# Clustered attention and a gated MLP: score and maxima matmuls over 128 partitions instead of 80 or 81, and a new list of operations

## The chip, the cores and the metric

The kernel runs on one core of a Trainium2 chip. The metric is the device time of one execution in microseconds (us). The core has TensorE (PE, with its weight loads shown apart as PEld), VectorE (DVE), ScalarE (ACT), GpSimd (POOL) and SyncE (SP), which issues nearly all transfers. Each engine works through its own queue in order.

## The reference

Four batches of eight heads with 768 positions of 64 dimensions. Each query and each key is put into one of 16 clusters (the nearest centroid by cosine). A query attends only to keys of its own cluster. The result goes through an MLP with a spatial gate.

```python
q_assign = np.argmax(np.einsum('bhsd,hcd->bhsc', q_n, c_n), axis=-1)
k_assign = np.argmax(np.einsum('bhsd,hcd->bhsc', k_n, c_n), axis=-1)
mask = q_assign[:, :, :, None] == k_assign[:, :, None, :]
scores = np.where(mask, scale * np.matmul(q, k.transpose(0, 1, 3, 2)), -1000000000.0)
attn = np.exp(scores - np.max(scores, axis=-1, keepdims=True))
attn = attn / (np.sum(attn, axis=-1, keepdims=True) + 1e-09)
x = np.matmul(attn, v)                 # heads side by side: (4, 768, 512)
h = np.maximum(x @ w_in, 0.0)
u, v = (h[..., :d_ff // 2], h[..., d_ff // 2:])
v_n = (v - mu) / np.sqrt(var + 1e-06)
v_s = np.einsum('ts,bsd->btd', w_spatial, v_n) + b_spatial[None, :, None]
out = (u * v_s) @ w_out
```

## The kernel before

The heads are taken in 16 pairs (four to a batch), and each head of a pair is a unit of attention. For a pair, `prep` (L604, for the first pair `prep0`, L546) loads keys and queries transposed (`raw`), splits them into a half-precision high part and a low part, and finds the clusters: small matmuls with the centroids (L570 to L572, L632 to L634, L644), then five VectorE steps (L664 to L669) and two that write a one-hot row for each cluster into `ohx` (L677, L678). SP transposes `ohx` into `oht` (L679) and copies its rows into the operand tile (L690).

That operand tile, `hq`, has 128 partitions and three slots of two heads by 768 positions. Slot 0 holds the keys' high part in partitions 0 to 63 and in 64 to 79 the keys' one-hot rows, partition 80 a constant row. Slot 1 holds the queries' high part, the queries' one-hot rows in 64 to 79, and from 80 on up to three shift rows, which are written later: they carry each query's maximum, so that the exponent needs no subtraction of its own. Slot 2 and the tile `lo` hold the operands with the low parts. Four tiles `hq` go round. The constants in the code are R_OH = 64, R_SH = 80, R_E = 81, R_END = 83.

For each unit, `shifts` (L739) forms the scores once to get the maxima: matmuls at L762 over partitions 0 to 79 (`0:R_SH`), each half (512 columns) or two quarters (2 x 256 columns) of a row block into one PSUM tile `acc`, of which there are four; VectorE reduces each to a maximum (L768). The maxima go as rows through `shx` and `sht` into `hq` (L795, L801; for the first pair through a matmul at L792). `attend` (L844) then forms the transposed scores: first the part with low parts over 128 partitions (L865), then the high part with one-hot and shift rows over 81 partitions (L867, `0:R_E`). ACT takes the exponent (L875) and the half-precision high part (L879), POOL the low part (L880), and TensorE sums with V (L885). Of the pairs 9, 11, 13 and 15 `attend_rows` (L806) does it by rows, without shifts: scores at L818 and L820 (the latter over 80 partitions), the maximum at L823.

When the four pairs of a batch are done, `mlp` (L942) follows: all its large matmuls are at L951, with 128 partitions and 512 columns, and fill TensorE beside the attention of the next batches.

The order is not made by a scheduler. The program first collects all operations with what they need, each with a number, and `Plan.run` issues them in the order of the list `ORDER` (L129, 3164 numbers). Each engine's queue, SP's included, is what that list leaves for it.

Of the kernel before, what the change touches and what calls it, by code (L numbers as in the profile page):

```python
# [8 lines left out]
F16 = mybir.dt.float16  # L9
# [6 lines left out]
P = 128  # L16
# [22 lines left out]
HQ_BUFS = 4  # L39
# [59 lines left out]
class Plan:  # L99
# [166 lines left out]
def kernel(  # L266
# [253 lines left out]
    def sp(fn, **k):  # L520
        return op("SP", fn, **k)
# [284 lines left out]
    def attend_rows(u):  # L806
# [5 lines left out]
        for t in range(NT):  # L812
# [3 lines left out]
            def scores(sc=sc, ts=ts):  # L816
                for cs in halves:
                    T.matmul(out=sc.t[:, cs], lhsT=hq.t[:, 2, h, ts], rhs=lo.t[:, h, cs], start=True, stop=False)  # L818
                for cs in halves:
                    T.matmul(out=sc.t[:, cs], lhsT=hq.t[0:R_SH, 1, h, ts], rhs=hq.t[0:R_SH, 0, h, cs], start=False, stop=True)  # L820
# [284 lines left out]
```

## Time and profile before

| | |
|---|---|
| median of 3 timed runs | 639.91 us (638.49 to 640.25) |
| the profiled execution, its own time | 643.21 us |
| span of its profile | 641.4 us |
| mean granted TensorE clock | 0.979 |
| DMA | 87.73 MB, mean 137 GB/s |
| costliest groups | POOL L880, 144 of 1706 ns; DVE L768, 216 of 681 ns; ACT L875, 144 of 900 ns; PE L951, 1296 of 379 ns |

A line of the profile names the engine, the line of the kernel, the operation, what it writes and reads, and its shape. Matmuls are pipelined: one of 512 columns lasts 379 ns by its record, but the next one starts earlier, so the distance from start to start tells its cost. "PEclk" is the share of its full clock that TensorE was granted. In a timeline the brackets at the end of a row give the idle time of the engine ahead of it and what ended it.

### The profile page before, as it was taken

How to read it: one execution, taken by the hardware profiler on the slowest of the kernel's cores; microseconds unless marked ns; L12 is line 12 of the kernel's file. 1: busy time of each engine (PE TensorE's matmuls, PEld its weight loads, DVE VectorE, ACT ScalarE, POOL GpSimd, SP SyncE). 2: the span in 40 equal slices, each digit the busy share in tenths (PEclk: the TensorE clock that was granted, in tenths of full speed). 3: DMA queues.
4: the chain of work that ended last, by engine and by line, in shares of the span. 5: the costliest groups of instructions: out<-in, count | busy, mean ns of one | idle time of the engine just before them, and what ended most of it. 6: DMA issues, size and time to landing. Idle time of an engine off the chain costs nothing.

```text
span 641.4 us, 16489 instructions
## 1 busy us (share of the span) xinstructions
PE 609.4 (95%) x6573; PEld 363.3 (57%) x6573; DVE 478.9 (75%) x994; ACT 446.6 (70%) x722; POOL 432.8 (67%) x309
## 2 busy tenths in 40 slices
PE   3889989889999999999999999999999999999997
PEld 2436666576666666546555575566556655544443
DVE  6997999999999997897779678669797665245220
ACT  6667989999987888747568587788769965022002
POOL 3453889998797889657657778588679887224210
PEclk9956999999999999999999999999999999999999
DMA  6556786677474656734989879888896189810145
GB/s 205 134 127 166 111 181 135 157 174 176 103 188 104 152 122 153 150 84 107 183 131 184 184 152 187 145 167 149 167 171 122 32 156 154 128 33 34 26 73 164
DMA packets 174812, 87.73 MB, mean 137 GB/s; under 512 B 158448, under 2 KB 161552, under 8 KB 174736
## 3 DMA queue, kind: packets, MB, share of 16 engines
q1 hardware_dynamic: 171136, 80.40, 62.0%
q10 hardware_dynamic: 3600, 6.30, 2.9%
q8 instruction: 51, 0.84, 0.6%
q14 instruction: 25, 0.20, 0.1%
HBM read 27.63 MB, written 6.29 MB: 53 GB/s over the span
## 4 chain that ended last, share of the span: by engine, by line
PE 72%; DVE 14%; ACT 4%; DMA 3%; issue 3%; POOL 1%; SPq 1%; ACTq 0%; DVEq 0%
PE acc L951 39%; PE acc L885 8%; PE acc L762 6%; DVE nm L768 5%; PE sc L865 5%; PE sc L867 5%; PE acc L834 4%; PE sc L818 2%; PE sc L820 2%; DMA xT<-wk 2%; DVE lo L544 1%; ACT wk L879 1%; DMA raw<-in_kqT_dram 1%; POOL wk L880 1%; ACT wk L875 1%
## 5 line engine op out<-in xcount | busy, mean ns | idle before, releaser
L880 POOL TENSOR_TENSOR wk<-wk,wk 128x768 f16<-128x768 f32 x144 | 242.4, 1706 | 42.7 <-ACT wk L879 30.7
L768 DVE TENSOR_REDUCE nm<-acc 128x1 f32<-128x512 f32 (+1 forms) x216 | 140.4, 681 | 25.3 <-PE acc L762 25.0
L875 ACT ACTIVATE wk<-sc,plog 128x768 f32<-128x768 f32 x144 | 127.7, 900 | 22.2 <-PE sc L867 16.5
L951 PE MATMUL acc<-win,xT 128*128 128x512 f16 x576 | 134.2, 379 | 0.1
L879 ACT CAST wk<-wk 128x768 f16<-128x768 f32 x144 | 116.7, 831 | 6.2 <-PE acc L885 3.4
L951 PE MATMUL acc<-vn,wsp 128*128 128x512 f16 x432 | 99.6, 379 | 1.0 <-DVE nm L768 0.9
L829 POOL TENSOR_TENSOR wk<-wk,wk 128x768 f16<-128x768 f32 x48 | 80.3, 1676 | 29.9 <-ACT wk L828 26.6
L885 PEld LDWEIGHTS <-wk 128*128 128x128 f16 x2592 | 90.1, 98 | 10.9 <-issue 1.1
L885 PE MATMUL acc<-vhl,wk 128*128 128x65 f16 (+1 forms) x2592 | 95.4, 194 | 0.2 <-POOL wk L880 0.2
L762 PE MATMUL acc<-hq 80*128 80x512 f16 (+1 forms) x288 | 82.4, 360 | 11.7 <-DVE nm L768 3.8
L951 PEld LDWEIGHTS <-xT 128*128 128x128 f16 x576 | 55.0, 97 | 62.1 <-issue 2.1
L865 PE MATMUL sc<-hq,lo 128*128 128x512 f16 (+1 forms) x288 | 72.5, 334 | 2.8 <-ACT wk L875 2.0
L867 PE MATMUL sc<-hq 81*128 81x512 f16 (+1 forms) x288 | 72.4, 333 | 0.0
L951 PEld LDWEIGHTS <-wsp 128*128 128x128 f16 x432 | 41.5, 98 | 47.9 <-issue 1.6
L823 DVE TENSOR_REDUCE nq<-sc 128x1 f32<-128x768 f32 x48 | 45.8, 954 | 28.8 <-PE sc L820 25.4
L951 PE MATMUL acc<-wou,wk 128*128 128x512 f16 x288 | 67.1, 379 | 0.0
L826 ACT ACTIVATE wk<-sc,nq 128x768 f32<-128x768 f32 x48 | 47.5, 990 | 24.6 <-DVE nq L825 5.8
L1014 POOL TENSOR_TENSOR wk<-u,wk 128x512 f16<-128x512 f32 x24 | 28.3, 1188 | 38.6 <-DVE wk L1013 34.6
L1012 DVE SCALAR_TENSOR_TENSOR u<-acc,bsp,u 128x512 f32<-128x512 f32 x24 | 17.8, 744 | 42.1 <-PE acc L951 42.1
L762 PEld LDWEIGHTS <-hq 80*128 80x128 f16 x288 | 27.7, 104 | 35.3 <-issue 20.4
L993 POOL TENSOR_TENSOR vn<-wk,vn 128x512 f16<-128x512 f32 x24 | 29.6, 1239 | 24.8 <-DVE vn L992 24.4
L951 PEld LDWEIGHTS <-wk 128*128 128x128 f16 x288 | 27.7, 97 | 31.4
(144 smaller groups left out, 881.1 us busy)
## 6 DMA issues: line engine op xcount, KB each, us to landing
raw<-in_kqT_dram SPq DMA_DIRECT2D x15, 768.0 KB
wk<-in_vp_dram SPq DMA_DIRECT2D x16, 384.0 KB
out_dram<-wk ACTq DMA_DIRECT2D x24, 256.0 KB
hq<-hq SPq DMA_DIRECT2D x15, 384.0 KB
hq<-lo SPq DMA_DIRECT2D x15, 192.0 KB
lo<-hq SPq DMA_DIRECT2D x15, 192.0 KB
wraw<-in_wsT_dram SPq DMA_DIRECT2D x12, 192.0 KB
vn<-in_w_in_dram SPq DMA_DIRECT2D x4, 512.0 KB
```

Of the source, the lines that this page charges most:

```text
L762: T.matmul(out=acc.t[:, i * w:(i + 1) * w], lhsT=hq.t[0:R_SH, 1, h, t * P:(t + 1) * P], rhs=hq.t[0:R_SH, 0, h, cs], start=i == 0, stop=i = ...
L768: V.tensor_reduce(out=cols(nm.t), in_=src, axis=AX.X, op=ALU.max, negate=True)
L823: o = op("DVE", lambda sc=sc, nq=nq: V.tensor_reduce(out=nq.t[:, 0:1], in_=sc.t[:, 0:S], axis=AX.X, op=ALU.max, negate=True), after=[o], u ...
L826: o = op("ACT", lambda sc=sc, p32=p32, nq=nq, t=t: A.activation(out=p32.t, in_=sc.t[:, 0:S], func=AF.Exp, bias=nq.t[:, 2:3], scale=nq.t[:, ...
L829: o = op("POOL", lambda pt=pt, p32=p32: G_.tensor_tensor(out=pt.t[:, 1, :], in0=p32.t, in1=pt.t[:, 0, :], op=ALU.subtract), after=[o], use ...
L865: T.matmul(out=sc.t[:, c:c + cs.stop - cs.start], lhsT=lo.t[:, h, ks], rhs=hq.t[:, 2, h, cs], start=True, stop=False)
L867: T.matmul(out=sc.t[:, c:c + cs.stop - cs.start], lhsT=hq.t[0:R_E, 0, h, ks], rhs=hq.t[0:R_E, 1, h, cs], start=False, stop=True)
L875: A.activation(out=p32.t, in_=sc.t[:, 0:S], func=AF.Exp, bias=plog, scale=SC_UNIT)
L879: o = op("ACT", lambda pt=pt, p32=p32: A.copy(out=pt.t[:, 0, :], in_=p32.t), after=[o], use=[p32], new=[pt])
L880: o = op("POOL", lambda pt=pt, p32=p32: G_.tensor_tensor(out=pt.t[:, 1, :], in0=p32.t, in1=pt.t[:, 0, :], op=ALU.subtract), after=[o], use ...
L885: T.matmul(out=av.t[:, j * AV_COLS:j * AV_COLS + w], lhsT=lhsT, rhs=rhs, skip_group_check=True, **f)
L951: T.matmul(out=acc.t, lhsT=lr[m][0], rhs=lr[m][1], start=(m == 0), stop=(m == n - 1))
```

## The change

The matmuls of the maxima (L762) and of the scores (L820, L867) read all 128 partitions of `hq` in place of 80 or 81. For this, what lies beyond must give zero: slot 1 is zeroed once in partitions 64 to 127 of each of the four tiles, by four memsets on POOL (`c_hq`), and the copies of the one-hot rows now bring 19 rows (`R_END - R_OH`) in place of 16 or 17, so that zeros also stand where the shift rows will come. Slot 0 keeps queries in partitions 83 to 127, which meet the zeros of slot 1. The four `hq` tiles become fixed tiles, so that the zeros stay. The sums computed are the same.

```diff
-    r_hq = R(ops, "hq", [P, 3, 2, S], F16, HQ_BUFS)
+    hqs = [ops.tile([P, 3, 2, S], F16, name="hq%d" % i, bufs=1) for i in range(HQ_BUFS)]
+    r_hq = R(None, "hq", None, None, HQ_BUFS, tiles=hqs)
...
+    c_hq = [op("POOL", lambda x=x: G_.memset(x[D:P, 1], 0.0)) for x in hqs]
...
-                m = C if a else C + 1
+                m = R_END - R_OH
...
-            m = C if x > 1 else C + 1
+            m = R_END - R_OH
...
-            rows.append(sp(lambda dst=dst, src=src: nc.sync.dma_start(out=dst(), in_=src()), after=[tr, lg] + qa0, use=[hq, oht]))
+            rows.append(sp(lambda dst=dst, src=src: nc.sync.dma_start(out=dst(), in_=src()), after=[tr, lg] + qa0 + c_hq[n:n + 1], use=[hq, oht]))
...
-                    T.matmul(out=acc.t[:, i * w:(i + 1) * w], lhsT=hq.t[0:R_SH, 1, h, t * P:(t + 1) * P], rhs=hq.t[0:R_SH, 0, h, cs], start=i == 0, stop=i == m - 1, skip_group_check=True)
+                    T.matmul(out=acc.t[:, i * w:(i + 1) * w], lhsT=hq.t[:, 1, h, t * P:(t + 1) * P], rhs=hq.t[:, 0, h, cs], start=i == 0, stop=i == m - 1, skip_group_check=True)
...
-                    T.matmul(out=sc.t[:, cs], lhsT=hq.t[0:R_SH, 1, h, ts], rhs=hq.t[0:R_SH, 0, h, cs], start=False, stop=True)
+                    T.matmul(out=sc.t[:, cs], lhsT=hq.t[:, 1, h, ts], rhs=hq.t[:, 0, h, cs], start=False, stop=True)
...
-                    T.matmul(out=sc.t[:, c:c + cs.stop - cs.start], lhsT=hq.t[0:R_E, 0, h, ks], rhs=hq.t[0:R_E, 1, h, cs], start=False, stop=True)
+                    T.matmul(out=sc.t[:, c:c + cs.stop - cs.start], lhsT=hq.t[:, 0, h, ks], rhs=hq.t[:, 1, h, cs], start=False, stop=True)
```

The list `ORDER` is made anew, with 3168 numbers. Its first line before and now:

```diff
-    0, 11, 13, 14, 4, 5, 8, 12, 9, 15, 16, 17, 18, 19, 20, 21, 22, 7, 1, 2, 3, 162, 163, 165,
+    0, 15, 4, 5, 16, 10, 17, 18, 7, 13, 9, 19, 20, 21, 22, 23, 24, 25, 26, 1, 167, 2, 3, 6,
```

Apart from the four memsets each engine has the same operations as before; they stand in another order. The lines of the changed kernel are one higher from L367 on and two higher from L434 on. Three places follow.

POOL at the start of the program, before: constants and the first tiles are set, then comes the norm of the centroids (`nrm`).

```order
L429 MEMSET ohx 128x768
L429 MEMSET ohx 128x6x2
L434 MEMSET vhl_89 128x12
L434 MEMSET vhl_90 128x12
L431 MEMSET shx_86 128x768
L431 MEMSET shx_86 128x6x2
L439 ISA
L439 TENSOR_TENSOR nrm<-ss,half 128x1
```

And now, where hq_130 is the tile of the first pair and hq_131 that of the second:

```order
L436 MEMSET vhl_89 128x12
L436 MEMSET vhl_90 128x12
L432 MEMSET hq_131 64x1536
L433 MEMSET shx_86 128x768
L433 MEMSET shx_86 128x6x2
L432 MEMSET hq_130 64x1536
L441 ISA
L441 TENSOR_TENSOR nrm<-ss,half 128x1
```

Two of the new memsets stand ahead of the norm, and the memset of `ohx` has gone behind it. The other two stand later: one ahead of the first L880 (L882 in the changed kernel), one behind the third.

DVE in the same stage, before: the end of the norm's chain, the low parts `lo` of the first pair's two heads, the centroids' low part `cmx`, and the first maximum of the clusters.

```order
L447 COPY wk_107<-wk_107 128x64
L428 MEMSET cmx 128x256
L544 SCALAR_TENSOR_TENSOR lo<-raw,hq 128x768
L459 TENSOR_TENSOR cmx<-acc_126,cmx 64x8x16 x2
L544 SCALAR_TENSOR_TENSOR lo<-raw,hq 128x768
L582 TENSOR_REDUCE mx<-acc_127 128x12
```

And now:

```order
L449 COPY wk_107<-wk_107 128x64
L428 CAST id_80<-wk_107 128x128
L546 SCALAR_TENSOR_TENSOR lo<-raw,hq_130 128x768
L461 TENSOR_TENSOR cmx<-acc_126,cmx 64x8x16 x2
L546 SCALAR_TENSOR_TENSOR lo<-raw,hq_130 128x768
L584 TENSOR_REDUCE mx<-acc_127 128x12
```

The memset of `cmx` went ahead of the norm's chain and a cast of the identity took its place; both `lo` still stand behind the chain.

SP around the one-hot rows of the second pair, before: the transposition of `ohx`, three copies for the first three pairs, and the rows.

```order
L679 DMA_TRANSPOSE oht<-ohx 128x6x128
L620 DMA hq<-lo 64x1536
L561 DMA hq<-lo 64x768
L619 DMA hq<-hq 64x2x1536
L690 DMA hq<-oht 16x768 x2
L690 DMA hq<-oht 17x768 x2
```

And now:

```order
L681 DMA_TRANSPOSE oht<-ohx 128x6x128
L621 DMA hq_132<-hq_132 64x2x1536
L577 DMA lo<-hq_130 64x768
L692 DMA hq_131<-oht 19x768 x4
```

Two copies stand between the transposition and the rows in place of three. The copy from `lo` into the second pair's tile went behind the rows.

More of the change, by code (lines that the diff above doesn't have):

```diff
@@ L598, in prep0 @@
                 tr = op("PE", lambda tp=tp, a=a, h=h: [T.matmul(out=tp.t[0:2 * C, t * P:(t + 1) * P], lhsT=oh0[:, t, 2 * a + h].rearrange("p e c -> p (e c)"), rhs=id16, start=True, stop=True) for t in range(NT)], after=[k, c_id], use=[sx], new=[tp])
-                X["rows"][h].append(op("ACT", lambda tp=tp, a=a, h=h, m=m: A.copy(out=hq.t[R_OH:R_OH + m, a, h, :], in_=tp.t[0:m, 0:S]), after=[tr, lg] + ([] if a else [qa, qb]), use=[hq, tp]))
+                X["rows"][h].append(op("ACT", lambda tp=tp, a=a, h=h, m=m: A.copy(out=hq.t[R_OH:R_OH + m, a, h, :], in_=tp.t[0:m, 0:S]), after=[tr, lg, c_hq[0]] + ([] if a else [qa, qb]), use=[hq, tp]))
             X["rows"][h].append(qa)
```

262 rows, old and new, of the table ORDER are left out of this document.

## The prediction

> **What bounds the kernel now.** I read the page first: the engines' shares, then the rows of 40 slices (16 us each).
>
> ```profile
> PE 609.4 (95%) x6573; PEld 363.3 (57%) x6573; DVE 478.9 (75%) x994; ACT 446.6 (70%) x722; POOL 432.8 (67%) x309
> DVE  6997999999999997897779678669797665245220
> PEclk9956999999999999999999999999999999999999
> ```
>
> TensorE is busy for 95% of the span, but its clock row shows 5 and 6 in the third and fourth slice. VectorE is at 9 from the third slice to the sixteenth with one exception. So there are stages. The second view is the table of stretches, cut where the granted clock changes. Its columns are the length, then busy time (and instructions) of PE, weight loads, DVE, ACT and POOL, then the clock, the DMA share and GB/s.
>
> ```profile
> 38.80:49.04 10.24, 10.14 (x32) 3.71 (x31) 9.77 (x17) 6.24 (x11) 9.51 (x6) 0.50 0.65 138
> 49.04:52.45 3.41, 3.41 (x12) 1.51 (x10) 2.83 (x7) 2.12 (x5) 0.18 (x1) 0.50 0.76 205
> 52.45:55.86 3.41, 3.41 (x14) 1.52 (x12) 2.48 (x5) 2.04 (x3) 0.00 (x0) 0.50 0.89 173
> 55.86:59.28 3.42, 3.42 (x48) 2.89 (x46) 3.42 (x5) 1.95 (x3) 2.13 (x2) 0.50 0.81 182
> 59.28:150.00 90.72, 82.62 (x1347) 59.52 (x1346) 85.12 (x166) 87.37 (x141) 80.96 (x53) 1.00 0.71 152
> 150.00:550.00 400.00, 395.72 (x4520) 240.88 (x4517) 317.45 (x644) 306.56 (x500) 305.64 (x206) 1.00 0.72 145
> ```
>
> Three stages follow. From 38.80 to 59.28 us TensorE has half its clock and is busy with hardly a pause. From 59.28 to 150 it has the full clock, and DVE (85.12 of 90.72) and ACT (87.37) are nearly full. From 150 to 550 TensorE is busy 395.72 of 400 us: it has the gated MLP's matmuls to fill with and sets the end. So whatever brings batch 0 forward before 150 us should move the end by as much; what is saved on other engines later should not.
>
> The third view is the chain that ended last, around the slow stretch.
>
> ```profile
> 38.49 2.80 PE acc L762 x7
> 48.65 0.64 PE sc L865 x2
> 58.62 0.64 PE sc L865 x2
> 59.66 0.33 PE sc L865 x2
> ```
>
> The chain lies on TensorE there, and the same two matmuls of a score take 0.64 us before the clock returns and 0.33 us after. The fourth view asks who fills the slow stretch: the maxima (L762, 80 partitions) and the sums with V (L885, mostly 128), each in the same stretches.
>
> ```profile
> 49.04:52.45 3.41, 2.34 (x6) 0.91 (x6) 0.50 0.76 205
> 55.86:59.28 3.42, 0.66 (x3) 0.19 (x2) 0.50 0.81 182
> 55.86:59.28 3.42, 2.54 (x42) 2.36 (x40) 0.50 0.81 182
> ```
>
> The first two rows are L762's, the last is L885's. TensorE was full from 49.04 to 55.86 and the clock stayed at 0.50; it came back at 59.28, right after the first stretch that held mostly 128-partition work. That is what one would see if the clock followed how many rows of the array work, not only whether TensorE is busy. The change sets exactly that. It is one transition, so it is a theory.
>
> [...]
>
> **The change part by part.** *128 in place of 80 or 81 partitions.* The nearest rows are two scores of the other attention form, 768 columns each, with 128 partitions (L818) and with 80 (L820), and the matmul behind them.
>
> ```profile
> 300.15 0.49 PE L818 MATMUL sc<-lo,hq 128*128 128x512 f16 x2
> 300.48 0.49 PE L820 MATMUL sc<-hq 80*128 80x512 f16 x2
> 300.81 0.38 PE L951 MATMUL acc<-wou,wk 128*128 128x512 f16 x1
> ```
>
> From start to start both take 0.33 us: the wider operand costs 0.
>
> *The clock.* What VectorE loses to a slow TensorE stands in its timeline, in the idle time ahead of each row.
>
> ```profile
> 39.11 0.69 DVE L768 TENSOR_REDUCE nm<-acc 128x1 f32<-128x512 f32 x1 [0.58 <-PE acc L762]
> 51.68 2.48 DVE L768 TENSOR_REDUCE nm<-acc 128x1 f32<-128x512 f32 x4 [0.54 <-PE acc L762]
> 55.09 0.69 DVE L768 TENSOR_REDUCE nm<-acc 128x1 f32<-128x512 f32 x1 [0.93 <-PE acc L762]
> 61.24 0.56 DVE L664 TENSOR_REDUCE mx<-acc 128x24 f32<-128x384 f32 x1 [1.93 <-PE acc L634]
> ```
>
> The last three are 0.54 + 0.93 + 1.93 = 3.4 us. TensorE's work from 48.65 to 59.28 would take half of 10.6 us at full clock, so it would be ahead of VectorE there, and the 3.4 us go. What is late next is VectorE itself, which is why the gain is 3.4 and not the 5.3 us that TensorE saves there. Bounds: 0, if the clock stays; above, 3.4 plus the 5.6 us that DVE is still idle from 59.28 to 150 (90.72 - 85.12), if those waits too come from work that started late: 9.0. I take 3.4, since only those rows name TensorE in the slow stretch.
>
> *Four memsets on POOL, two of them at the start.* Each zeroes 64 x 1536 halves. Here are the sizes shown, and the start of POOL and DVE.
>
> ```profile
> L431 POOL MEMSET shx<- 128x768 f16 x1 | 0.8, 780 | 0.0
> L432 POOL MEMSET mean<- 128x132 f16 x2 | 0.4, 208 | 0.0
> 1.11 0.95 POOL L429 MEMSET ohx<- 128x768 f16 x2
> 1.96 0.22 POOL L434 MEMSET vhl<- 128x12 f16 x2
> 2.03 0.99 POOL L431 MEMSET shx<- 128x768 f16 x2
> 3.16 0.57 POOL L439 TENSOR_TENSOR nrm<-ss,half 128x1 f32<-128x1 f32 x1
> 3.76 0.15 DVE L441 TENSOR_SCALAR ninv<-nrm 128x1 f32<-128x1 f32 x1 [0.24 <-POOL nrm L439]
> 5.46 0.94 DVE L544 SCALAR_TENSOR_TENSOR lo<-raw,hq 128x768 f16<-128x768 f32 x1
> 6.43 0.59 DVE L459 TENSOR_TENSOR cmx<-acc,cmx 64x128 f16<-64x128 f32 x2
> 8.01 0.96 DVE L544 SCALAR_TENSOR_TENSOR lo<-raw,hq 128x768 f16<-128x768 f32 x1 [0.99 <-ACT hq L555]
> ```
>
> (780 - 208) / (768 - 132) = 0.90 ns a column, so 1536 columns take 780 + 768 x 0.90 = 1470 ns; bounds 0.78 us (if the count of elements sets it) and 1.56. The order puts two ahead of the centroids' norm and moves the memset of ohx (1.96 - 1.11 = 0.85 us of POOL's queue) behind it. POOL is then free at 3.02 - 0.85 + 2 x 1.47 = 5.11 in place of 3.02, and the norm starts 1.95 us later. VectorE's chain of the norm, the first lo and cmx behind it are in one queue: cmx ends at 7.02 + 1.95 = 8.97. The second lo used to wait 0.99 us for ACT until 8.01, so it starts 0.96 us late, and the rest of the start hangs on it. I take +1.0; bounds 0 (0.78 us each) and +1.15 (1.56). The other two memsets stand around POOL's first L880s, in a stretch where POOL waits:
>
> ```profile
> 38.98 1.64 POOL L880 TENSOR_TENSOR wk<-wk,wk 128x768 f16<-128x768 f32 x1 [6.52 <-ACT wk L879]
> 57.15 5.07 POOL L880 TENSOR_TENSOR wk<-wk,wk 128x768 f16<-128x768 f32 x3 [7.93 <-ACT wk L879]
> ```
>
> That idle time hides 2 x 1.47 = 2.9 us; without cover they cost that.
>
> *The rows' DMAs.* Pair 1's four one-hot rows were issued third behind the transposition; now they are second.
>
> ```profile
> 28.81 1.34 SPq L679 DMA_TRANSPOSE oht<-ohx  x1
> 30.20 0.58 SPq L620 DMA_DIRECT2D hq<-lo  x1
> 30.82 0.59 SPq L561 DMA_DIRECT2D hq<-lo  x1
> 31.52 0.62 SPq L619 DMA_DIRECT2D hq<-hq  x1
> 32.24 3.37 SPq L690 DMA_DIRECT2D hq<-oht  x4
> ```
>
> Two issues stand between instead of three: -0.6 us on the way to the maxima at 38.49, whose lateness is the 0.58 us of VectorE above. That nineteen rows go where 16 or 17 did I count at 0; at worst it takes the 0.6 back (bounds -0.6 and 0).
>
> *The list made anew elsewhere.* TensorE's idle time from 150 to 550 is 400 - 395.72 = 4.3 us; a better list can win no more than that there, a worse one might lose about as much. I take 0, since the counts of instructions are unchanged.
>
> *The sum.* -3.4 + 1.0 - 0.6 = -3.0 us. The profiled execution took 643.21 us (its span 641.4): it would be 640.2. That execution lies 3.3 us above the median of the three timed runs, 639.91, so against the median: 636.9.
>
> **The rivals.** *A, no clock gain.* The gate counts busy time or instructions, not rows (the lifting stretch also had 48 matmuls in place of 12). Then zeros change nothing: +1.0 - 0.6, or 640.3. For it: the evidence is one transition, and DVE and ACT are full anyway until 150 us. [...] Against it: the two full windows without effect. 0.26.
>
> *B, slower.* The four memsets meet a POOL without slack: +1.15 at the start, and both later ones delay the low halves (L880) on which the sums with V wait, +2.9: 639.9 + 4.1 = 644.0. It decides once ACT's casts come early enough that the waits of 6.52 and 7.93 us are gone and no clock gain reaches the end. Against it: POOL has 90.72 - 80.96 = 9.8 us free up to 150. 0.18.
>
> *C, more.* The clock comes back earlier, and the list also fills TensorE's 4.3 us: -3.0 - 4.3, or 632.6. Against it: nothing in the counts of work says so. 0.10.
>
> **How the numbers follow.** Forecast 0.46, with a range of its own of 634.5 to 639. A measurement can tell 0.3% from no change, here 1.9 us, so faster means below 638.0 and slower above 641.8. Nine tenths of the forecast's case (0.42) and C make 0.52; A and the rest of the forecast make 0.30; B makes 0.18. The range goes down to 631.5, a little beyond C, and up to 643.0: it leaves out the upper half of B (0.09) and some of C.
>
> **What would show it.** The clock row should lose its 5 and 6 in slices three and four, or keep only one stretch of 3 to 7 us at half. Score pairs should take 0.33 us by 50 us, and VectorE's waits on L762 and L634 between 50 and 62 should vanish. The norm on POOL should start near 5.1 us, and the second lo near 9.0. The first MLP matmuls (L951) should come about 3 us earlier than in the profile of before. The step is wrong if the clock stays at 0.50 up to some 59 us although every matmul there has 128 partitions, or if it returns and VectorE is still last by the same amount at 150 us.

## The result, and the profile after

The changed kernel takes 645.82 us (median of 6 runs, 644.04 to 647.75), the kernel before 639.9 us beside it (6 runs): ratio 1.0097, 95% interval 1.0073 to 1.0121. It is slower by 1%, where 636.9 was predicted and the range ended at 643.0. The profiled execution has a span of 646.0 us against 641.4, 4.6 us more. These two executions lie 1.9 us (changed) and 3.3 us (before) above the medians of their kernels, so a mark read from a single execution may be off by some 3 us.

Rows of the page of the changed kernel: the engines' shares, the clock by slices, and the row of the maxima's matmuls (L764, which was L762).

```profile
PE 602.9 (93%) x6573; PEld 361.1 (56%) x6573; DVE 473.1 (73%) x994; ACT 448.5 (69%) x722; POOL 435.4 (67%) x313
PEclk9978889999999999999999999999999999999999
PE 67%; DVE 9%; DMA 8%; ACT 7%; POOL 4%; issue 3%; SPq 1%; ACTq 0%; DVEq 0%; POOLq 0%
L764 PE MATMUL acc<-hq 128*128 128x512 f16 (+1 forms) x288 | 77.8, 348 | 18.9 <-DMA hq<-oht 10.5
```

The clock row has lost its 5 and 6, as predicted, and TensorE's busy time fell from 609.4 to 602.9 us. Yet the span grew, so TensorE is idle longer. The last row says where: 18.9 us of idle time ahead of the maxima, most of it behind the transfer `hq<-oht`, the copies of the one-hot rows. Transfers hold 8% of the chain that ended last (third row; 3% before).

The chain of waits of the changed kernel, around the first four pairs (start, length, what):

```profile
34.23 5.70 DMA hq<-oht
39.93 0.09 issue
40.02 0.60 PE acc L764
...
46.93 5.65 DMA hq<-oht
...
73.54 4.96 DMA hq<-oht
...
110.90 5.75 DMA hq<-oht
```

Four times the chain waits 5 to 6 us for the one-hot rows; before, the chain up to 180 us held one such step:

```profile
35.01 3.34 DMA hq<-oht
```

The table of stretches of the changed kernel, with the columns of the prediction:

```profile
38.80:45.60 6.80, 4.74 (x15) 1.97 (x16) 5.02 (x10) 3.28 (x7) 5.14 (x4) 0.75 0.75 97
45.60:52.50 6.90, 3.67 (x19) 1.41 (x18) 6.23 (x12) 3.89 (x6) 1.61 (x2) 1.00 0.41 135
52.50:59.30 6.80, 6.61 (x63) 4.02 (x64) 6.22 (x10) 4.07 (x8) 1.71 (x3) 0.75 0.81 191
72.90:90.00 17.10, 13.38 (x144) 8.65 (x142) 12.50 (x26) 12.20 (x22) 13.10 (x9) 0.80 0.51 131
150.00:550.00 400.00, 393.60 (x4483) 240.42 (x4482) 318.78 (x649) 312.62 (x508) 307.45 (x209) 1.00 0.75 146
```

The fourth of them in the kernel before:

```profile
72.90:90.00 17.10, 15.21 (x215) 10.19 (x213) 16.58 (x35) 16.74 (x25) 16.57 (x11) 1.00 0.81 154
```

TensorE was busy with hardly a pause from 38.80 to 59.28; now it stands idle for 2.1 and 3.2 us in the first two stretches and 3.7 in the fourth, where it was 1.9 before. In 72.90 to 90 it is not TensorE alone: VectorE and ACT are busy 12.50 and 12.20 us, where they were busy 16.58 and 16.74. The chain puts 4.96 us of that stretch down to the copies. The first MLP matmul, the mark of how far batch 0 has come, starts at 157.0 us and not at 152.0 (the first numbers after the durations):

```profile
L951 PE MATMUL acc<-win,xT x576: 376/379/391, 152.0 to 611.4; 128*128 128x512 f16 x192
L953 PE MATMUL acc<-win,xT x576: 376/379/390, 157.0 to 618.6; 128*128 128x512 f16 x192
```

In these two executions the 5.0 us lost before the MLP begins are the whole loss of the span, 4.6 us.

Why do the copies land late? SP issues them earlier than before, at 31.69 in place of 32.24, as the prediction had it. What grew is the time behind the issue. SP's row of the four issues, and two stretches of the changed kernel in which hardly any other transfer is under way:

```profile
31.69 3.11 SPq L692 DMA_DIRECT2D hq<-oht  x4
34.50:35.50 1.00, 1.00 (x4) 0.38 (x3) 0.97 (x4) 1.00 (x2) 0.00 (x0) 0.50 0.07 25
38.50:39.50 1.00, 0.00 (x0) 0.00 (x0) 0.36 (x2) 1.00 (x2) 0.79 (x1) 1.00 0.10 34
```

In the first stretch the share of the 16 transfer engines is 0.07, about one in sixteen (0.06), at 25 GB/s. The packet records show single rows of 1536 bytes there, one behind another at 61 ns (1536 bytes in 61 ns are 25 GB/s). Four copies of 19 rows, one row at a time, are 76 x 0.061 = 4.6 us. In the trace of before the second pair has both kinds side by side: the 32 rows of its two copies of 16 start within 0.61 us (34.67 to 35.28), several under way at a time, and the 34 rows of its two copies of 17 go one behind another in 2.50 us (35.55 to 38.05), most of them 61 ns apart. The semaphores of the second pair's copies tell the two kinds apart too: each of 16 rows steps its semaphore 16 times (before), each of 17 (before) or 19 rows (changed) twice. What sets whether the rows of a copy go together or one by one is not shown by these two traces; the experiments below try 20, 31 and 32 rows.

### The profile page after: what moved, and what is told of

The parts are those of the page before. It is cut to its first block, busy times and chain, and to the rows that moved or that the text cites. A ratio compares the mean times of both kernels' runs of the same rounds, so it can differ in the third digit from the quotient of the medians.

```text
span 646.0 us, 16462 instructions
## 1 busy us (share of the span) xinstructions
PE 602.9 (93%) x6573; PEld 361.1 (56%) x6573; DVE 473.1 (73%) x994; ACT 448.5 (69%) x722; POOL 435.4 (67%) x313
## 4 chain that ended last, share of the span: by engine, by line
PE 67%; DVE 9%; DMA 8%; ACT 7%; POOL 4%; issue 3%; SPq 1%; ACTq 0%; DVEq 0%; POOLq 0%
PE acc L953 37%; PE acc L887 8%; PE acc L764 5%; PE sc L867 4%; PE sc L869 4%; DMA hq<-oht 3%; DVE nm L770 3%; PE acc L836 3%; DMA wk<-wk 3%; POOL wk L882 2%; ACT wk L877 2%; PE sc L820 2%; ACT wk L881 2%; PE sc L822 2%; DMA wraw<-in_w_out_dram 2%
## 5 line engine op out<-in xcount | busy, mean ns | idle before, releaser
L882 POOL TENSOR_TENSOR wk<-wk,wk 128x768 f16<-128x768 f32 x144 | 240.9, 1696 | 54.2 <-ACT wk L881 53.6
L953 PE MATMUL acc<-win,xT 128*128 128x512 f16 x576 | 133.5, 379 | 1.0 <-DVE nm L770 1.0
L953 PE MATMUL acc<-vn,wsp 128*128 128x512 f16 x432 | 100.4, 379 | 1.0 <-DVE nm L770 1.0
L764 PE MATMUL acc<-hq 128*128 128x512 f16 (+1 forms) x288 | 77.8, 348 | 18.9 <-DMA hq<-oht 10.5
L953 PEld LDWEIGHTS <-xT 128*128 128x128 f16 x576 | 55.0, 98 | 62.4 <-issue 1.5
L867 PE MATMUL sc<-hq,lo 128*128 128x512 f16 (+1 forms) x288 | 71.9, 332 | 2.6 <-ACT wk L877 2.5
L869 PE MATMUL sc<-hq 128*128 128x512 f16 (+1 forms) x288 | 71.6, 331 | 0.0
L953 PEld LDWEIGHTS <-wsp 128*128 128x128 f16 x432 | 41.4, 98 | 47.0 <-issue 1.8
L953 PE MATMUL acc<-wou,wk 128*128 128x512 f16 x288 | 66.4, 379 | 0.0
L828 ACT ACTIVATE wk<-sc,nq 128x768 f32<-128x768 f32 x48 | 47.6, 991 | 21.8 <-DVE nq L827 12.5
L764 PEld LDWEIGHTS <-hq 128*128 128x128 f16 x288 | 27.1, 102 | 39.8 <-issue 18.5
L953 PEld LDWEIGHTS <-wk 128*128 128x128 f16 x288 | 27.8, 98 | 31.1
```

The lines of the kernel that those rows point to most:

```text
L764: T.matmul(out=acc.t[:, i * w:(i + 1) * w], lhsT=hq.t[:, 1, h, t * P:(t + 1) * P], rhs=hq.t[:, 0, h, cs], start=i == 0, stop=i == m - 1, s ...
L828: o = op("ACT", lambda sc=sc, p32=p32, nq=nq, t=t: A.activation(out=p32.t, in_=sc.t[:, 0:S], func=AF.Exp, bias=nq.t[:, 2:3], scale=nq.t[:, ...
L867: T.matmul(out=sc.t[:, c:c + cs.stop - cs.start], lhsT=lo.t[:, h, ks], rhs=hq.t[:, 2, h, cs], start=True, stop=False)
L869: T.matmul(out=sc.t[:, c:c + cs.stop - cs.start], lhsT=hq.t[:, 0, h, ks], rhs=hq.t[:, 1, h, cs], start=False, stop=True)
L882: o = op("POOL", lambda pt=pt, p32=p32: G_.tensor_tensor(out=pt.t[:, 1, :], in0=p32.t, in1=pt.t[:, 0, :], op=ALU.subtract), after=[o], use ...
L953: T.matmul(out=acc.t, lhsT=lr[m][0], rhs=lr[m][1], start=(m == 0), stop=(m == n - 1))
```

## The experiments

In the expectations T1 is the theory that the copies of 19 rows cause the loss, since their rows go one behind another; T2, the first rival, is that the new list does. The runs' times stand beside the kernel before on the same chip (639.9 to 641.3 us); ratios are against it.

**Copies of 32 rows (e1).** The changed kernel with 32 rows copied in place of 19. The 13 rows more are zeros of the same operand in `oht`; the shift rows are written later, as before.

```diff
-            m = R_END - R_OH
+            m = 2 * C
```

> The changed kernel with one edit: the four copies of one-hot rows of a pair bring 32 rows each (the 16 one-hot rows and the 16 rows behind them, of which those beyond the first three are zeros) in place of 19; same result. Theory T1: a copy of 16 rows goes to many DMA engines at once, one of 17 or 19 rows goes row after row (the packets of the changed kernel follow each other at 61 ns, four copies of 19 rows are 76 x 0.062 = 4.7 us, where before two copies of 17 were 34 x 0.062 = 2.1 us); the pair's maxima (L764) wait for it. Then TensorE's waits on hq<-oht fall from 10.5 us to under 3 us and the time from 645.8 to between 636 and 641 us. Theory T2: the list made anew orders the work worse. Then the time stays at 644 to 647. Theory T3: the two memsets ahead of the norm cost the time (up to 2 us at the start). Then it also stays within 1 us of 645.8.

Measured: 635.25 us, ratio 0.9899 (0.9872 to 0.9926). With more bytes moved, the kernel is 10.6 us faster than the changed one and faster than before. The waits of TensorE for these copies (total, times, longest), in the changed kernel and then in e1:

```profile
PE acc L764 <- DMA hq<-oht: 10.5, 4, 3.7
PEld L764 <- DMA hq<-oht: 4.1, 1, 4.1
```

```profile
PEld L764 <- DMA hq<-oht: 1.6, 1, 1.6
PE acc L764 <- DMA hq<-oht: 1.2, 1, 1.2
```

They fall from 14.6 to 2.8 us, by 11.8: about the time won. And three stretches of e1:

```profile
45.60:52.50 6.90, 5.92 (x33) 3.15 (x33) 6.87 (x14) 5.05 (x9) 2.77 (x2) 0.87 0.39 82
52.50:59.30 6.80, 6.80 (x154) 5.53 (x153) 6.80 (x12) 6.59 (x10) 4.42 (x4) 1.00 0.83 206
150.00:550.00 400.00, 399.26 (x4505) 243.12 (x4504) 308.82 (x642) 304.77 (x497) 303.45 (x206) 1.00 0.73 148
```

Here is what the prediction forecast: the full clock by 52.5 us, VectorE full (6.80 of 6.80), and later TensorE idle for 0.7 of 400 us where it was 4.3 before. The first MLP matmul starts at 148.7 us, 3.3 earlier than in the kernel before:

```profile
L953 PE MATMUL acc<-win,xT x576: 376/379/390, 148.7 to 604.2; 128*128 128x512 f16 x192
```

The span of e1 is 631.5 us, 9.9 less than before, so in these executions a third of the gain is made ahead of the MLP and the rest behind it.

**80 and 81 partitions again (e2).** The changed kernel with its list, memsets and 19 rows; only the operands of the matmuls (L764, L822, L869) are cut as before; the diff shows the first and the last.

```diff
-  lhsT=hq.t[:, 1, h, t * P:(t + 1) * P], rhs=hq.t[:, 0, h, cs]
+  lhsT=hq.t[0:R_SH, 1, h, t * P:(t + 1) * P], rhs=hq.t[0:R_SH, 0, h, cs]
...
-  lhsT=hq.t[:, 0, h, ks], rhs=hq.t[:, 1, h, cs]
+  lhsT=hq.t[0:R_E, 0, h, ks], rhs=hq.t[0:R_E, 1, h, cs]
```

> The changed kernel with the matmuls of scores and maxima set back to 80 and 81 partitions; list, memsets and copies of 19 rows stay; same result. If the granted clock follows how many partitions work: the clock falls to half for one stretch of 15 us or more between 30 and 70 us, as before the change, its mean falls from 0.987 to under 0.982, and the time goes up from 645.8 to 647 to 651 us. If the clock follows busy time alone: the same three or four short stretches at half as in the changed kernel, mean 0.987, time 645.8 within 1 us.

Measured: 650.6 us, ratio 1.0148 (1.0122 to 1.0174), 0.5% above the changed kernel. The same score (the seventh of the program) in TensorE's timeline, in e2 and then in the changed kernel, and a stretch of e2:

```profile
51.21 0.85 PE L867 MATMUL sc<-hq,lo 128*128 128x512 f16 x2
51.85 0.85 PE L869 MATMUL sc<-hq 81*128 81x512 f16 x2
```

```profile
49.46 0.49 PE L867 MATMUL sc<-hq,lo 128*128 128x512 f16 x2
49.78 0.49 PE L869 MATMUL sc<-hq 128*128 128x512 f16 x2
```

```profile
45.60:52.50 6.90, 6.84 (x23) 2.46 (x21) 6.90 (x13) 2.84 (x4) 1.13 (x1) 0.50 0.43 142
```

In e2 TensorE is busy 6.84 of 6.90 us and has half its clock; the changed kernel, busy only 3.67 us there, has the full clock. In e2 the half clock lasts in one piece from 41.37 to 61.85 us, by the records of the granted clock. Only the operands differ, and in the changed kernel the half clock lasts only from 39.80 to 43.21 and from 53.45 to 56.86 us between 38.80 and 59.30: in these two executions the clock went with the partitions that the matmuls read, zeros included. The waits for the copies moved as well; e6 below makes the same test without them.

**The old list (e3).** The changed kernel's operations in the order of the list of before, the four memsets right behind the norm (numbers 9 to 12 behind 19).

```diff
-    0, 15, 4, 5, 16, 10, 17, 18, 7, 13, 9, 19, 20, 21, 22, 23, 24, 25, 26, 1, 167, 2, 3, 6,
+    0, 15, 17, 18, 4, 5, 8, 16, 13, 19, 9, 10, 11, 12, 20, 21, 22, 23, 24, 25, 26, 7, 1, 2,
```

> The changed kernel with the list of before the change, the four memsets put right behind the norm on POOL, where POOL is idle for 6.9 us; 128 partitions and copies of 19 rows stay; same result. T1 (copies of 19 rows): the waits on hq<-oht stay at 6 us or more and the time at 642 to 647. T2 (the list): 636 to 640, as the forecast had it. T3 (memsets ahead of the norm): about 2 us under the changed kernel, 643.5 to 644.5.

Measured: 652.6 us, ratio 1.0191 (1.0159 to 1.0223), slower than each of the theories had it. The new list is not the cause; it takes some of the harm away. The row of L764 in the page of e3:

```profile
L764 PE MATMUL acc<-hq 128*128 128x512 f16 (+1 forms) x288 | 78.4, 343 | 25.7 <-DMA hq<-oht 13.9
```

**The kernel before with 32 rows (e4).** If slow copies were all, the kernel before should gain as well: half of its copies had 17 rows.

```diff
-            m = C if x > 1 else C + 1
+            m = C if x > 1 else 2 * C
```

> The kernel of before the change with one edit: the two copies of the keys' rows of a pair bring 32 rows in place of 17 (the rows beyond are read by no matmul); same result. T1: the last packet of a pair's rows lands about 2 us sooner, TensorE's waits on hq<-oht fall from 3.6 us to under 2, and the time from 639.9 to between 636.5 and 639.3. If the number of rows doesn't matter: 639.9 within 0.7 us, or a little more for the larger copies.

Measured: 640.65 us (12 runs), ratio 0.9987 (0.9964 to 1.0009): not the gain expected, and none that can be told. Two stretches of e4:

```profile
38.80:45.60 6.80, 6.67 (x22) 2.34 (x22) 6.80 (x12) 4.30 (x9) 6.25 (x4) 0.50 0.76 193
45.60:52.50 6.90, 6.90 (x22) 3.07 (x21) 6.32 (x13) 4.14 (x8) 3.24 (x3) 0.50 0.58 151
```

The rows come sooner (TensorE's waits for them are 2.3 us, 4.2 before), but TensorE is busy 6.67 of 6.80 and 6.90 of 6.90 us at half clock, so it would be last in their place. That is a reading and not shown: in the profiled execution of e4 the first MLP matmul starts at 148.9 us, 3.1 earlier than in that of the kernel before, and the span is 637.7 us, 3.7 less, though the medians show no gain.

**Copies of 31 rows (e5).** One row fewer than e1.

```diff
-            m = R_END - R_OH
+            m = 2 * C - 1
```

> The changed kernel with copies of 31 rows in place of 19 (the rows beyond 19 are zeros); same result. One row less than the copies of 32, which landed within 1.0 to 2.0 us of their last issue. T1 (a number of rows that has no common divisor with the sixteen engines goes row after row): 4 x 31 x 0.062 = 7.7 us per pair, last packet 7 us or more after the last issue, and the time goes up from 645.8 to 655 to 670 us. If 32 rows gained by something else than an even spread (their size, or what they overwrite): like the copies of 32, 633 to 638 us.

Measured: 673.77 us (4 runs), ratio 1.0539 (1.049 to 1.0587), more than expected. The chain of waits of e5 and its waits for these copies:

```profile
34.53 8.36 DMA hq<-oht
...
49.91 8.21 DMA hq<-oht
...
78.33 8.50 DMA hq<-oht
```

```profile
PE acc L764 <- DMA hq<-oht: 27.9, 7, 6.9
PEld L764 <- DMA hq<-oht: 9.0, 2, 7.3
```

Against e1 the waits grew by 36.9 - 2.8 = 34 us and the time by 38.5. From the second pair to the sixth the packets of four such copies end 7.0 to 7.6 us behind the last issue; 4 x 31 x 0.061 is 7.6, about what 124 rows take one by one. That the divisor decides, as T1 has it, is not shown.

**32 rows, with 80 and 81 partitions (e6).** The edits of e1 and e2 together.

> Copies of 32 rows as in the run before, the list made anew, and the matmuls of scores and maxima set back to 80 and 81 partitions; same result. It tells what the partitions alone are worth once the copies are quick. If the clock follows the partitions and VectorE was held up by it as the prediction has it (3.4 us): half clock for 17 us or more between 30 and 65 us, and 638 to 641 us, some 3 to 5 us above the 635.25 with 128 partitions. If the clock gains nothing at the end: 635 within 1 us, though the clock record gets worse.

Measured: 639.82 us (12 runs), ratio 0.9984 (0.9967 to 1.0001). Against e1 only the operands differ. Two stretches of e6, to be read beside those of e1:

```profile
45.60:52.50 6.90, 6.87 (x25) 3.06 (x24) 6.86 (x14) 4.35 (x8) 2.75 (x2) 0.50 0.35 97
52.50:59.30 6.80, 6.80 (x55) 3.99 (x53) 5.54 (x9) 4.68 (x8) 2.81 (x3) 0.55 0.86 197
```

TensorE is busier than in e1 from 45.60 (6.87 against 5.92) and has the lower clock (0.50 against 0.87); from 52.50 it does 55 matmuls in the time in which e1 does 154. Rival A of the prediction ("the gate" is its word for what grants the clock) had the clock follow busy time or the number of matmuls. Here is the stretch of e1 at whose end the clock came back, and one of the same length in e6 at whose end it did not (it came back at 58.63):

```profile
43.93:47.35 3.42, 3.38 (x14) 1.28 (x13) 3.42 (x6) 0.79 (x1) 1.64 (x1) 0.50 0.57 185
48.39:51.81 3.42, 3.42 (x13) 1.67 (x12) 3.38 (x8) 3.04 (x6) 0.86 (x1) 0.50 0.10 24
```

Busy time and count are as good as equal (3.38 us and 14 matmuls, 3.42 us and 13), so neither tells them apart.

**32 rows, the old list (e7).** The edits of e1 and e3 together.

> 128 partitions, copies of 32 rows, the list of before the change with the four memsets right behind the norm; same result. It tells what the list made anew is worth once the copies are quick. If the old list is as good and only the copies spoiled the change: 633 to 637 us. If the list made anew was needed for the gain: 638 to 643 us. Under the copies of 19 rows the old list was 6 us slower than the new one, with more waits on the copies (13.9 us against 10.5), so I lean to the first.

Measured: 638.46 us (12 runs), ratio 0.9968 (0.9944 to 0.9991). The leaning of the expectation was wrong: the new list was needed. The clock comes back about as in e1 (0.89 from 45.60 to 52.50 us), and the first MLP matmul starts at 147.2 us, but in 150 to 550 us TensorE is busy no longer than before:

```profile
150.00:550.00 400.00, 395.72 (x4478) 240.78 (x4477) 315.01 (x641) 302.49 (x495) 304.67 (x207) 1.00 0.73 148
```

**32 rows, and the memsets behind the norm (e8).** e1 with the first two memsets (9 and 10) behind the norm (19).

```diff
-    0, 15, 4, 5, 16, 10, 17, 18, 7, 13, 9, 19, 20, 21, 22, 23, 24, 25, 26, 1, 167, 2, 3, 6,
+    0, 15, 4, 5, 16, 17, 18, 7, 13, 19, 9, 10, 20, 21, 22, 23, 24, 25, 26, 1, 167, 2, 3, 6,
```

> The changed kernel with copies of 32 rows and the two first memsets put right behind the norm instead of ahead of it; same result. The norm then starts near 2.3 to 3.2 us in place of 5.27 and VectorE's second low part about 1 us sooner. If the start carries through to the end: 0.8 to 1.5 us below the 635.25 of the run with copies of 32 rows alone. If the later stages take it up: the same within 0.7 us.

Measured: 632.73 us, ratio 0.9877 (0.9846 to 0.9907), the best of all kernels here and ahead of both. Against e1 it is 0.0022 less, 1.4 us, within the intervals. The norm on POOL starts at 3.18 us, where 5.27 was. The second `lo` on VectorE, in the changed kernel (e1 has the same row) and then in e8:

```profile
9.26 0.96 DVE L546 SCALAR_TENSOR_TENSOR lo<-raw,hq 128x768 f16<-128x768 f32 x1 [0.15 <-ACT hq L557]
```

```profile
8.47 0.96 DVE L546 SCALAR_TENSOR_TENSOR lo<-raw,hq 128x768 f16<-128x768 f32 x1 [0.15 <-ACT hq L557]
```

It comes 0.79 us earlier.

**Copies of 20 rows (e9).** One row more than the changed kernel.

```diff
-            m = R_END - R_OH
+            m = R_END - R_OH + 1
```

> The changed kernel with copies of 20 rows in place of 19, one row more, nothing else; same result. If the copies are spread over as many engines as divide the number of rows (20 rows: ten engines, two rows each; 19: one engine), the last packet lands within about 2.5 us of the last issue, as with 32 rows, and the time is 633 to 638 us. If only multiples of 16 rows are spread, 80 packets go one after another, 5 us, and the time is 645 to 649, as with 19 rows or a little above. [...]

Measured: 633.78 us (4 runs), ratio 0.9902 (0.9868 to 0.9935). One row more in each copy takes 12 us off the changed kernel. The waits of e9 are those of e1:

```profile
PEld L764 <- DMA hq<-oht: 1.6, 1, 1.6
PE acc L764 <- DMA hq<-oht: 1.3, 1, 1.3
```

From the second pair to the sixth the copies end 0.9 to 1.6 us behind the last issue, where 80 rows at 61 ns would take 4.9. The time is that of the first case of the expectation; how many engines share a copy of 20 rows, which that case names, is not shown.

## Why the prediction was wrong

**The step that failed** is the term of the rows' DMAs: "That nineteen rows go where 16 or 17 did I count at 0; at worst it takes the 0.6 back (bounds -0.6 and 0)". The first half of the term was right: the issue came 0.55 us earlier, 0.6 said. The growth of the copies was then put at 0 without a reason; how a copy's rows are carried was not asked. Time from the end of the last issue of a pair to its last packet, worked out from the packet records, for the second to the sixth pair (us):

```
before, 2 x 16 and 2 x 17 rows   2.44  2.36  1.96  1.95  1.94
after,  4 x 19 rows              4.83  4.74  4.15  5.01  5.18
e9,     4 x 20 rows              0.94  0.94  1.56  0.93  0.95
e1,     4 x 32 rows              1.02  1.42  1.60  1.55  1.02
e5,     4 x 31 rows              7.43  7.00  7.53  7.60  7.42
```

(The 5.18 is the time at which the semaphore of the copies was full, since packets of other transfers lie among theirs.) For the second pair the term is 4.83 - 2.44 = +2.4 us in place of 0, and it returns with each pair. Over the kernel, the difference of the ratios of the changed kernel and e9 gives it: (1.0097 - 0.9902) x 640 = 12.5 us, give or take 2.7. With quick copies (e9) the change is worth 0.0098 x 640 = 6.3 us, where the sum said 3.0, so other terms were off as well, the other way. The rows were there to be read before: two of the four copies of the kernel before already had 17 rows, and its chain held 3.34 us of `hq<-oht` at 35.01. I had asked of that step when it was issued, not what it takes per row.

**The clock, -3.4.** That the clock would come back sooner was right: from 45.60 to 52.50 us it was 0.87 in e1, while in e6 6.87 of 6.90 us busy, much of it at 80 and 81 partitions, left it at 0.50. The size depends on what is late next. Between e2 and the changed kernel it is (1.0148 - 1.0097) x 640 = 3.3 us, between e6 and e1 (0.9984 - 0.9899) x 640 = 5.4, each give or take 2. In the changed kernel the clock also falls again near TensorE's waits for the slow copies: score pairs in the changed kernel take 0.84 us at 54.21, behind a wait for the copies.

```profile
52.67 1.74 PE L764 MATMUL acc<-hq 128*128 128x512 f16 x7 [2.40 <-DMA hq<-oht]
54.21 0.84 PE L867 MATMUL sc<-hq,lo 128*128 128x512 f16 x2
57.47 0.49 PE L867 MATMUL sc<-hq,lo 128*128 128x512 f16 x2
```

**The memsets, +1.0.** The start of POOL in the changed kernel:

```profile
3.81 1.37 POOL L432 MEMSET hq<- 64x1536 f16 x1
5.27 0.57 POOL L441 TENSOR_TENSOR nrm<-ss,half 128x1 f32<-128x1 f32 x1
```

1.37 us for a memset (1.47 estimated), the norm at 5.27 (5.11) and the second `lo` at 9.26 (9.0; 8.01 before), 1.25 us later, a little past the bound of 1.15: the step holds about where it can be seen. At the end of the kernel e8 wins 1.4 us by undoing it, which its interval can't tell from 0. The two later memsets were hidden, as said: POOL waits 5.56 us for ACT behind the last one.

**The list, 0.** Too pessimistic. Between e7 and e8, both with the first two memsets behind the norm, it is worth (0.9968 - 0.9877) x 640 = 5.8 us, give or take 2.5; with 19 rows, between e3 and the changed kernel, 6.0 us. Where it is won is less plain. TensorE's idle time from 150 to 550, 4.3 us before, is 0.7 in e1 and 1.2 in e9, as rival C had described, but 3.9 in e8, which is as fast. The span less the start of the first MLP matmul, in one execution of each kernel, is 489.4 us before, 489.0 in the changed kernel, 488.8 in e4 and 488.6 in e7; with the new list and quick copies it is 482.8 (e1), 483.4 (e9), 486.2 (e6) and 486.8 (e8). In e3 and e5, where the chain waits for late copies behind it too, it is 491.9 and 495.8. So the stretch behind that start grew shorter only where the new list and quick copies came together. Rival C got 0.10 because I argued from counts of instructions, which say nothing of waits.

**The rivals.** None was the case. B had the side right and the mechanism wrong: POOL was not what was late. The missing rival was a transfer that gets slower although it hardly grows. **The marks** told it well: the clock row and the score pairs at 0.33 us from start to start by 50 us came out as said, while VectorE kept waits on L764 of 1.22 and 0.71 us (at 53.08 and 61.21) and L953 came 5.0 us later, not 3 earlier. One reading of the prediction was off, with nothing resting on it: the row of VectorE falls to 7 in the fourth slice and in the sixteenth, two exceptions and not one.

**Why each part alone shows so little.** With quick copies (20 or 32 rows) the old list with 80 partitions gives 0.9987 (e4), the new list alone 0.9984 (e6), the 128 partitions alone 0.9968 (e7), and both together 0.9899 to 0.9902 (e1, e9). From 0.9987 the two alone add up to -0.0022, together they give -0.0088; the difference, 0.0066, is give or take 0.0045, and the four kernels differ in their memsets too. So the terms don't seem to add. One explanation, not shown, is that with half clock TensorE is last and a better order can't help it, and that with the old order other engines are last and a faster TensorE can't help them. The change is worth 1% when its copies have 20 rows, and costs 1% when they have 19.

What stays open: why TensorE has half its clock in e1 too, from 33.69 to 37.11 and from 40.52 to 47.35 us by the records, where nearly all its matmuls use 128 partitions. Between the two it was busy only 1.62 of 3.41 us. In the second, 3.25 of 3.41 us busy did not bring the full clock and the next 3.38 of 3.42 did; what tells these two apart is not shown, and no run was made on it. Whether e8 beats e1 is open as well.

## What to carry to other kernels

Price a small copy by how many of its rows go one behind another in the trace, not by its bytes: before a count of rows is changed, look at what the copies of before take behind their last issue (here 1.9 to 2.4 us, with 19 rows 4.2 to 5.2), and try other counts as well, moving rows that nobody needs if one is quicker (here 20 and 32 rows took 0.9 to 1.6). When a change removes one wait, ask of each transfer in front of the same instruction whether the change touches it, even if only by two rows. When two edits each show nothing, try them together before dropping either.

## What the runs showed of the hardware

- Copies of 17 and 19 rows of 1536 bytes from tile to tile went row by row at 61 ns (with 19 rows at a share of 0.07 of the transfer engines, about one in sixteen), while the 32 rows of two copies of 16 started within 0.61 us (before). From the second pair to the sixth, four copies of 20 or 32 rows ended 0.9 to 1.6 us behind their last issue, four of 19 rows 4.2 to 5.2, four of 31 rows 7.0 to 7.6 (124 x 0.061 is 7.6). From 19 rows to 20 the kernel's time fell by 12 us, from 31 to 32 by 38.5.
- The granted clock of TensorE went with the number of partitions that its matmuls read, zeros included: with 80 and 81 it stayed at 0.50 through 6.87 us of work in 6.90 (e6), with 128 it was 0.87 in the same stretch with 5.92 us of work (e1). In 3.42 us, 14 matmuls and 3.38 us of work were followed by the full clock with 128 partitions (e1), 13 matmuls and 3.42 us of work with mostly 80 and 81 were not (e6).
- In the changed kernel half-clock stretches of 3.4, 3.4 and 6.8 us (from the records of the granted clock) began at 39.80, 53.45 and 77.34 us, each within idle times of TensorE of 3.42, 2.40 and 3.72 us that ended at 40.02, 52.67 and 78.55, or 0.8 us behind them. So in this execution a late copy went along with a slower clock for what came behind it.
